# Engine queues of a seven-product FFN: written-out order from the seventh step on, data preparation over two steps, more squares on ScalarE

## The chip, the core and the metric

The program runs on one core of a Trainium2 chip. The metric is the device time of one execution in microseconds. Three runs of the kernel before gave 1070.18, 1069.46 and 1069.93 us, so the median is 1069.93 us.

## What is computed

From q, k, v of 6080 tokens by 256 channels an attention over channels is computed, and its output goes through two feed-forward blocks of width 2048. All inputs are float32.

```python
qn = q / (norm(q, axis=1) + 1e-06);  kn = k / (norm(k, axis=1) + 1e-06)
a = softmax(kn.T @ qn / tau)                 # 256 x 256
x = v @ a                                    # 6080 x 256
x = square(relu(x @ w_in)) @ w_out           # first block, 256 -> 2048 -> 256
h = x @ w_in2
return (h * clip(h + 3, 0, 6) / 6) @ w_out2  # second block
```

## The kernel before

**Head.** The scores of q and k are summed while their pieces arrive, then come norms, softmax and the transposed attention matrix (functions `score`, `scaled`, `transposed`, lines 558 to 677). The attention is not applied to the tokens: `attn_w` (line 475) multiplies it into the first block's input weights, so that the first block reads v itself.

**Steps.** The body is a list of 96 steps (`order`, line 911): two blocks (`ph`), six chunks of tokens (`c`), four units of 512 hidden channels (`u`) and two halves of a unit (`p`). In this document a step is named by its index i, from 0 to 95; "the seventh step" is i = 6, the first that works on unit 3 of chunk 0. A step (`step`, line 752) computes the hidden values of its half unit for one chunk as a 2 by 2 block product and, beside that, issues 24 matmuls that multiply the hidden values of the step before with the output weights (`out_mms`, line 696).

- Steps 0 to 5 (unit number under `PLAIN` = 3 in chunk 0) are plain: four blocks of two products each. A block's values go from PSUM (tile s) through relu into r (L802), are squared into h (by ScalarE, L804, or by VectorE, L806), and are split into a high and a low part g (ScalarE L108, VectorE L111).
- From step 6 on a step takes seven products, M1 to M7 in the code, of sums of weight blocks and sums of data blocks. Each product is three matmuls (L767: high by high, high by low, low by high). M1, M6, M7 and M4 add up in one PSUM bank x. After M1 its value is copied to m1 (trace: m), after M6 to u2 and after M7 to u3 (trace: u, twice in a step), all three by ScalarE (L108). So M6 can't start before copy m has read the bank, M7 not before the first copy u, and M4 not before the second.

```python
mul(x, M1, True); copy_act(m1, x)            # L867, L868
run(before); carry[0](); carry[1](); beside(0)
mul(pp, M2, True); add(h11, m1, pp); carry[2]()
mul(y, M5, True); pop(pops[0]); act(h11, "1"); beside(1)
mul(x, M6, False); copy_act(u2, x); hi11(); beside(2); lo11(); pop(pops[1]); beside(3)
mul(x, M7, False); copy_act(u3, x); add(h22, u3, y); act(h22, "2"); beside(4); pop(pops[2])
mul(x, M4, False); act_psum(h21, x); hi22(); beside(5); lo22(); pop(pops[3])
mul(y, M3, False); hi21(); beside(6); add(h12, u2, y); lo21(); pop(len(outs))
```

`carry` is what the step before left over: relu and square of its h12, and the split of it. `act(h, b)` (line 788) squares on ScalarE (relu L791, square L792) where the table `SQUARED_BY_ACT` names b for that step, and on VectorE otherwise (L794, one instruction).

**What sets the order.** Every engine runs its own queue in the order in which the instructions stand there. TensorE, SyncE and GpSimd have program order throughout. For ScalarE and VectorE a scheduler orders the queue up to step `MANUAL_FROM` - 1 (line 47, 8 before); from there on they too have program order (line 971), which is the order of the code above. `beside` (line 772) puts in work for later: `background` takes it from a list of tasks with due steps (weights that are converted, L138 and L139 on ScalarE, L126, L130, L142 and L134 on VectorE, then split into oh and ol; weight sums, tile wblk, with due steps `SUMS_DUE`), and `lane` holds the next chunk's data: eight slots b that are split in the same way, and four sums of blocks (tile blk) that VectorE makes (`FIRST` and `REST`, line 436; `add_lane`, line 444). `pops`, a table of four numbers, says how many of the 24 output matmuls go between the products; from `MANUAL_FROM` on it is `POPS_2`.

Of the kernel before, what the change touches and what calls it, by code (L numbers as in the profile page):

```python
# [43 lines left out]
LANE = (0, 1, 0, 1, 1, 1, 1)  # L44
DUE = (5, 4)
FINE = True
MANUAL_FROM = 8
LOAD_AHEAD = (2, 8, 8)
PLAIN = 3
PLAIN_POPS = (7, 6, 4, 7)  # L50
SUMS_DUE = (8, 10, 11)
HELD_BEHIND = {("t", 0, 0): 3, ("w", 0, 3): 3, ("s", 0): 5, ("s", 1): 5, ("s", 2): 5}
LANE_BEHIND = 5
SPLIT_FROM = 2
POPS = (3, 7, 5, 4)
POPS_2 = (3, 5, 6, 5)
AW_POPS = (1, 1, 1, 1)
FIRST_POPS = (6, 7, 4, 7)
SQUARED_BY_ACT = ("1", "012", "1", "012", "1", "1", "12", "12")


@with_exitstack
def tile_channel_attention_then_two_ffn(
# [21 lines left out]
    chunks, s = [], 0  # L85
# [117 lines left out]
    def run(fs):  # L203
        for f in fs:
            f()
# [53 lines left out]
    def front(n, k=0):  # L259

        for _ in range(n):
            t = tasks[k]
            t.steps.pop(0)()
            done[0] += 1
            if not t.steps:
                finished.add(tasks.pop(k).name)
                ensure_loads()
# [168 lines left out]
    FIRST, REST = (1, 2, 0, "sums", 5, 4), (3, 6)  # L436
# [7 lines left out]
    def add_lane(ph, c, slots, due):  # L444
        assert not lane
        b_ops.setdefault((ph, c), {})
        lane.extend(data_prep(data[ph, c], chunks[c][1], slots, new_slot(ph, c)))
        lane_due[0] = due
# [26 lines left out]
    def attn_w(u):  # L475

        if u == 1:

            ps = [psy.tile([P, 512], F32, tag=f"y0{dh}", name="aw") for dh in range(2)]
        else:  # L480
            ps = [bank([P, 512]) for _ in range(2)]

        def product(dh, eh):
            if u < SPLIT_FROM:
                return lambda: PE.matmul(ps[dh], e_sb[dh][:, eh], w1[u][:, eh], start=(eh == 0), stop=(eh == 1))

            def f():
                for k, (x, y) in enumerate(((0, 0), (0, 1), (1, 0))):
                    PE.matmul(ps[dh], e_parts[dh][x][:, eh], w1[u][y][:, eh], start=(eh, k) == (0, 0), stop=(eh, k) == (1, 2))
            return f  # L490

        r = blocks_tile("wblk" if u < 2 else "st")
        data["w", u] = r

        def take(dh):
            def f():
                ACT.activation(out=r[:, dh:4:2], in_=ps[dh].rearrange("p (g f) -> p g f", g=2),
                               func=AF.Copy, scale=rsum[:, dh:dh + 1])
            return f
        return [product(dh, eh) for dh in range(2) for eh in range(2)], [take(dh) for dh in range(2)]  # L500
# [16 lines left out]
    with tc.tile_pool(name="qk", bufs=4) as qkp, tc.tile_pool(name="at", bufs=1) as atp:  # L517
# [51 lines left out]
        for i, (wide, j, g) in enumerate(pieces):  # L569
            if i:  # L570
                load_piece(i + 3)
            t = loaded[i]
# [18 lines left out]
            for b in range(0, g - m, width):  # L591
                w = min(width, g - m - b)
# [56 lines left out]
        def transposed(dh):  # L649
            for eh in range(2):  # L650
                PE.transpose(t_ps[dh][:, eh], sc[dh][:, eh * P:(eh + 1) * P], ident)
            if dh == 0:
                copy_act(e_sb[dh], t_ps[dh])
            else:
                gate.append(DVE.tensor_scalar(out=e_sb[dh], in0=t_ps[dh], scalar1=1.0, scalar2=None, op0=ALU.mult).ins)
# [10 lines left out]
        front(1)  # L666
        scaled(1)
        row_sum(0)
        front(3)
        run(products[:2])  # L670
        transposed(1)
        ahead, take_next = attn_w(1)
        run(ahead[:1])
        parts[2]()
# [77 lines left out]
    def step(i, ph, c, u, p, before, outs, carry):  # L752
# [19 lines left out]
        def beside(at):  # L772
            parts = BESIDE if i < MANUAL_FROM else BESIDE_2
            k = -(-todo[0] * parts[at] // max(1, sum(parts[at:])))
# [103 lines left out]
        mul(y, M5, True)  # L878
        pops = AW_POPS if i == 0 else POPS if i < MANUAL_FROM else POPS_2
        pop(pops[0])  # L880
# [31 lines left out]
    LAST = 2 * NU - 1  # L912
# [21 lines left out]
    for i, (ph, c, u, p) in enumerate(order):  # L934
        at = i % (LAST + 1)
        nxt = (ph, c + 1) if c + 1 < NCHUNK else (1, 0) if ph == 0 else None
        if ph == 0 and c == 0:
            if i == 0:
                add_out_1(1, 3)
            elif p == 1 and u + 1 < NU and u:  # L940
                add_out_1(u + 1, i + 2)
        if i == 1:
            need(("half o", 0))
            last_lo[2] = last_lo[0].ins
            held.extend([("s", 0), ("w", 0, 1)])
        if (ph, c) == (0, 1) and at == 0:
            end = i
            for x, f in [(x, f) for x in range(NU) for f in (add_in_2, add_out_2)]:
                end += DUE[f is add_out_2]
                f(x, end)  # L950
        if nxt and at == (2 if i > LAST else 6):
            add_lane(*nxt, FIRST, i - at + LAST)
        if at == 0:
            assert not lane
        if ph == 0:
            need(("w", ph, u))
            if PLAIN <= u and c == 0:
                need(("t", 0, 0))
            if c == 1 and u < PLAIN:
                need(("s", u))  # L960
        outs = []
        if not prev:
            need(("w1", 1))
            take = take_next
            outs = [(f, None) for f in ahead[1:]]
        else:
            if prev[0][0] == 0 and prev[0][1] == 0:
                if i > 1:
                    need(("o", prev[0][2]))
            outs = out_mms(*prev[0], prev[1])  # L970
        if i == MANUAL_FROM:
            phase[0] = 2
            ctx.enter_context(tc.manual_schedule())

        if nxt and at == LAST:
            add_lane(*nxt, REST, i + 1)
        g, carry = step(i, ph, c, u, p, before, outs, carry)
        if i == 1:
            first_hi = last_lo[1]
        before = []  # L980
        if nxt and at == (0 if i > LAST else 5):
            if i <= LAST:
                need(("t", 0, 0))
            load_data(*nxt)
        if ph == 0 and c == 0 and p == 0 and u + 1 < NU:
            need(("w1", u + 1))
            if u:
                if u + 1 == SPLIT_FROM:
                    with tc.issue_after(first_hi), tc.issue_after(last_lo[2]):
                        split_e()  # L990
                products, before = attn_w(u + 1)
                run(products)
            else:
                before = take
            add_task(("w", 0, u + 1), lambda x=u + 1: in_1_steps(x), i + 2)
        if ph == 0 and c == 0 and u < PLAIN:
            if p == 0 and u == PLAIN - 1 < NU - 1:
                add_data("t", 0, 0, ("sums", 5, 4, 3, 6), i + 2)
            elif p == (u < NU - 1):
                add_weight_sums(u, SUMS_DUE[u])  # L1000
        if ph == 0 and c == NCHUNK - 1 and p:
            fetch_2("w", u)
        if prev and prev[0][0] == 0 and prev[0][1] == NCHUNK - 1 and prev[0][3]:
            fetch_2("o", prev[0][2])
        prev = ((ph, c, u, p), g)
# [38 lines left out]
```

## Time and profile before

| | |
|---|---|
| median of three runs | 1069.93 us |
| the profiled execution's own time | 1071.04 us |
| its span (first to last instruction) | 1069.3 us |
| TensorE busy with matmuls | 1061.4 us (99%) |
| VectorE busy | 898.6 us (84%) |
| ScalarE busy | 647.9 us (61%) |
| share of TensorE in the chain that ended last | 90% |
| granted TensorE clock, mean | 0.999 |

Busy time is the sum of the instructions of an engine. A matmul is shown as busy from its start to its modelled end, and the matmuls overlap, so a TensorE that is "99% busy" is read better by the starts of its matmuls: in steps without a wait they are 0.23 us apart. In the timeline PE is a matmul, PEld its weight load, ACT is ScalarE, DVE is VectorE; the first number is the start, the second the duration, in us.

### The profile page before, as it was taken

What the parts mean: (1) busy time and instruction counts of PE and PEld (TensorE: products, weight loads), DVE (VectorE), ACT (ScalarE), POOL (GpSimd) and SP (SyncE); (2) the same over time, 40 slices, a digit from 0 to 9 for tenths busy, and PEclk for the clock granted to TensorE, in tenths of its full rate; (3) what the DMA queues carried; (4) which work ended last, traced back from release to release, by engine and by line L of the source; (5) the groups of instructions that cost most, each with busy time, mean ns of one, the idle gap of its engine ahead of it and who ended that gap; (6) DMA issues with size and microseconds to landing.
All of it is one profiled execution on the core that took longest, in us unless ns stands there. A gap on an engine that the chain in (4) does not pass through costs nothing.

```text
span 1069.3 us, 12813 instructions
## 1 busy us (share of the span) xinstructions
PE 1061.4 (99%) x4602; PEld 865.2 (81%) x4602; DVE 898.6 (84%) x1523; ACT 647.9 (61%) x1125; POOL 9.4 (1%) x22
## 2 busy tenths in 40 slices
PE   9999999999999999999999999999999999999998
PEld 8778787888888888888888888888888888888886
DVE  6899988977887987887868988898898898898785
ACT  7698886666666666666565455455545555555443
POOL 0000000000000000000100000000000000000000
PEclk9999999999999999999999999999999999999999
DMA  9623130223132114115435002002002002001001
GB/s 359 245 80 118 59 117 21 89 81 96 60 108 79 49 60 142 35 60 197 148 130 184 1 0 78 1 1 78 1 1 78 1 1 64 15 0 39 1 1 39
DMA packets 33567, 78.03 MB, mean 73 GB/s; under 512 B 3296, under 2 KB 16864, under 8 KB 33504
## 3 DMA queue, kind: packets, MB, share of 16 engines
q1 hardware_dynamic: 27024, 57.49, 16.2%
q0 software_dynamic: 2304, 11.54, 3.2%
q10 hardware_dynamic: 4176, 8.19, 2.1%
q8 instruction: 36, 0.59, 0.2%
q14 instruction: 27, 0.22, 0.1%
HBM read 53.22 MB, written 23.99 MB: 72 GB/s over the span
## 4 chain that ended last, share of the span: by engine, by line
PE 90%; DVE 3%; ACT 3%; DMA 2%; issue 1%; ACTq 0%; SPq 0%; DVEq 0%
PE y L709 47%; PE s L767 41%; PE sc L559 2%; DMA q<-q_dram 1%; DMA w<-w_out_dram 1%; DVE g L111 0%; ACT g L108 0%; DVE h L806 0%; DVE ct L142 0%; DVE accq L114 0%; ACT cv L139 0%; ACT u L108 0%; ACT ct L138 0%; DVE cv L134 0%; DVE b L111 0%
## 5 line engine op out<-in xcount | busy, mean ns | idle before, releaser
L709 PE MATMUL y<-g,oh 128*128 128x506 f32 (+1 forms) x1536 | 508.8, 392 | 0.0
L767 PE MATMUL s<-b,wh 128*128 128x506 f32 (+1 forms) x1356 | 422.9, 393 | 1.1 <-ACT m L108 0.8
L111 DVE TENSOR_TENSOR g<-h,g 128x506 fp32r<-128x506 f32 (+1 forms) x384 | 262.0, 683 | 94.9 <-ACT g L108 85.3
L709 PEld LDWEIGHTS y<-g,oh 128*128 128x128 f32 x1536 | 289.4, 188 | 64.3 <-DVE g L111 0.4
L767 PEld LDWEIGHTS s<-b,wh 128*128 128x128 f32 x1356 | 254.6, 188 | 62.0 <-ACT u L108 2.2
L709 PE MATMUL y<-g,ol 128*128 128x506 f32 (+1 forms) x768 | 302.0, 393 | 0.0
L767 PE MATMUL s<-b,wl 128*128 128x506 f32 (+1 forms) x678 | 265.9, 392 | 0.1
L108 ACT ACTIVATE g<-h 128x506 fp32r<-128x506 f32 (+1 forms) x384 | 235.1, 622 | 30.0 <-DVE h L815 14.3
L108 ACT ACTIVATE u<-s 128x506 f32<-128x506 f32 (+1 forms) x180 | 107.0, 595 | 135.5 <-PE s L767 135.5
L709 PEld LDWEIGHTS y<-g,ol 128*128 128x128 f32 x768 | 144.6, 188 | 31.7
L767 PEld LDWEIGHTS s<-b,wl 128*128 128x128 f32 x678 | 127.9, 189 | 28.7 <-DVE wl L111 0.6
L114 DVE TENSOR_TENSOR h<-u,s 128x506 f32<-128x506 f32 (+1 forms) x180 | 122.1, 678 | 25.4 <-ACT u L108 22.4
L108 ACT ACTIVATE m<-s 128x506 f32<-128x506 f32 (+1 forms) x90 | 53.6, 595 | 111.5 <-PE s L767 110.5
L798 DVE SCALAR_TENSOR_TENSOR h<-r,h 128x506 f32<-128x506 f32 (+1 forms) x144 | 98.9, 687 | 4.9
L794 DVE SCALAR_TENSOR_TENSOR h<-h 128x506 f32<-128x506 f32 (+1 forms) x122 | 83.2, 682 | 1.4
L814 ACT ACTIVATE r<-s,three 128x506 f32<-128x506 f32 (+1 forms) x48 | 32.9, 686 | 60.2 <-PE s L767 59.8
L114 DVE TENSOR_TENSOR h<-m,s 128x506 f32<-128x506 f32 (+1 forms) x90 | 61.2, 680 | 8.6 <-PE s L767 2.9
L797 DVE TENSOR_SCALAR r<-h 128x506 f32<-128x506 f32 (+1 forms) x144 | 60.6, 421 | 1.7
L111 DVE TENSOR_TENSOR b<-blk,b 128x506 fp32r<-128x506 f32 (+1 forms) x85 | 57.7, 680 | 0.0
L108 ACT ACTIVATE b<-blk 128x506 fp32r<-128x506 f32 (+1 forms) x85 | 51.9, 616 | 0.0
L811 ACT ACTIVATE r<-s 128x506 f32<-128x506 f32 (+1 forms) x42 | 25.0, 595 | 38.7 <-PE s L767 36.4
L815 DVE SCALAR_TENSOR_TENSOR h<-r,s 128x506 f32<-128x506 f32 (+1 forms) x48 | 32.7, 681 | 10.4 <-ACT r L814 10.3
(96 smaller groups left out, 510.7 us busy)
## 6 DMA issues: line engine op xcount, KB each, us to landing
w<-w_in_dram SPq DMA_DIRECT2D x16, 512.0 KB, 5.6
w<-w_out_dram SPq DMA_DIRECT2D x16, 512.0 KB, 3.8
k<-k_dram SPq DMA_DIRECT2D x10, 512.0 KB, 7.0
blk<-vT_dram SPq DMA_DIRECT2D x8, 506.0 KB, 6.4
y<-y ACTq DMA_DIRECT2D x16, 253.0 KB, 2.7
blk<-y SPq DMA_DIRECT2D x8, 506.0 KB, 5.0
outT_dram<-y SPq DMA_DIRECT2D x15, 253.0 KB, 2.1
q<-q_dram SPq DMA_DIRECT2D x7, 512.0 KB, 7.7
```

Of the source, the lines that this page charges most:

```text
L108: return ACT.activation(out=out, in_=in_, func=AF.Copy)
L111: return DVE.tensor_tensor(out=out, in0=a, in1=b, op=ALU.subtract)
L114: DVE.tensor_tensor(out=out, in0=a, in1=b, op=ALU.add)
L559: return lambda: PE.matmul(s_ps[dh][:, :C], t["k"][:, b, dh * P:(dh + 1) * P], t["q"][:, b], start=first, stop=last)
L709: PE.matmul(y_ps[ph, c, b, e][:, :n], w[:, j, e * P:(e + 1) * P], x, start=start, stop=stop)
L767: PE.matmul(dst, w[:, a, rows], x, start=first and k == 0, stop=k == 2, skip_group_check=True)
L794: DVE.scalar_tensor_tensor(out=h, in0=h, scalar=0.0, in1=h, op0=ALU.max, op1=ALU.mult)
L797: DVE.tensor_scalar(out=r, in0=h, scalar1=3.0, scalar2=0.0, op0=ALU.add, op1=ALU.max)
L798: DVE.scalar_tensor_tensor(out=h, in0=r, scalar=6.0, in1=h, op0=ALU.min, op1=ALU.mult)
L811: ACT.activation(out=r, in_=x, func=AF.Relu)
L814: ACT.activation(out=r, in_=x, func=AF.Relu, bias=three)
L815: DVE.scalar_tensor_tensor(out=h, in0=r, scalar=6.0, in1=x, op0=ALU.min, op1=ALU.mult)
```

## The change

Four constants are changed, one function is called with other arguments, and one instruction of the head moves.

- `MANUAL_FROM` goes from 8 to 6: program order on ScalarE and VectorE, and `POPS_2`, hold from step 6.
- The first entry of `SUMS_DUE` goes from 8 to 5, and that task loses its mark in `HELD_BEHIND`: the weight sums of unit 0 come in steps 1 and 2.
- For chunk 1 all eight slots are put on the lane at step 6 and are due at step 8; before, six of the entries were due at the end of step 6 and the last two in step 7.
- `SQUARED_BY_ACT`: steps 4 and 5 square one more value on ScalarE, and so do steps 6 and 7 (h12, "0").
- In the head, two of three preparation instructions stand ahead of a pair of products and the transposes, and one behind.

```diff
-MANUAL_FROM = 8
+MANUAL_FROM = 6
...
-SUMS_DUE = (8, 10, 11)
-HELD_BEHIND = {("t", 0, 0): 3, ("w", 0, 3): 3, ("s", 0): 5, ("s", 1): 5, ("s", 2): 5}
+SUMS_DUE = (5, 10, 11)
+HELD_BEHIND = {("t", 0, 0): 3, ("w", 0, 3): 3, ("s", 1): 5, ("s", 2): 5}
...
-SQUARED_BY_ACT = ("1", "012", "1", "012", "1", "1", "12", "12")
+SQUARED_BY_ACT = ("1", "012", "1", "012", "12", "12", "012", "012")
...
         row_sum(0)
-        front(3)
+        front(2)
         run(products[:2])
         transposed(1)
+        front(1)
         ahead, take_next = attn_w(1)
...
         if nxt and at == (2 if i > LAST else 6):
-            add_lane(*nxt, FIRST, i - at + LAST)
+            add_lane(*nxt, FIRST if i > LAST else FIRST + REST, i - at + LAST + (i <= LAST))
...
-        if nxt and at == LAST:
+        if nxt and at == LAST < i:
             add_lane(*nxt, REST, i + 1)
```

In the changed file the lines from 672 on have numbers that are one higher, so L792 there is L791 here. Three places show how the queues move. Names keep their buffer numbers here, as several tiles would read alike without: m1, u2, u3, h11, h12 and h22 are the tiles of the code above, r the relu, s a PSUM bank, b a slot of the next chunk's data, blk the raw data, ct and cv steps of a weight's conversion, wblk weight sums.

ScalarE in step 6, before: from copy m to the second copy u.

```order
L108 ACTIVATE m1_1172<-s_1175 128x508
L108 ACTIVATE oh_1187<-cv_1227 128x512
L791 ACTIVATE r_1203<-h11_1168 128x508
L108 ACTIVATE u2_1173<-s_1175 128x508
L792 ACTIVATE h11_1168<-r_1203 128x508
L108 ACTIVATE b_1263<-blk_1165 128x508
L108 ACTIVATE g_1215<-h11_1168 128x508
L108 ACTIVATE u3_1174<-s_1175 128x508
```

The same stretch in the changed kernel, from the instruction behind copy m on.

```order
L803 ACTIVATE r_1190<-s_1132 128x508
L108 ACTIVATE g_1193<-h12_1056 128x508
L792 ACTIVATE r_1210<-h11_1178 128x508
L793 ACTIVATE h11_1178<-r_1210 128x508
L108 ACTIVATE b_1213<-blk_1173 128x508
L108 ACTIVATE u2_1183<-s_1185 128x508
L108 ACTIVATE g_1220<-h11_1178 128x508
L108 ACTIVATE oh_1222<-cv_1163 128x512
L138 ACTIVATE ct_1232<-w64_1171 128x512
L139 ACTIVATE cv_1233<-w64_1171 128x512
L108 ACTIVATE b_1238<-blk_1173 128x508
L108 ACTIVATE u3_1184<-s_1185 128x508
```

The relu of step 5's last value (r_1190) and its split now stand behind copy m; relu and square of h11 and a slot b stand between copy m and the first copy u, and five instructions between the two copies u, where two and three stood.

VectorE at the start of step 6, before: from the end of step 5's values to the sum h11 that reads copy m.

```order
L806 TENSOR_TENSOR h22_1050<-r_1109 128x508
L142 ISA ct_1226<-ct_1226,cv_1227 128x1024
L134 SCALAR_TENSOR_TENSOR cv_1227<-w64_1163,ct_1226 128x512
L111 TENSOR_TENSOR g_1112<-h22_1050,g_1112 128x508
L806 TENSOR_TENSOR h12_1048<-r_1180 128x508
L111 TENSOR_TENSOR b_1206<-blk_1165,b_1206 128x508
L111 TENSOR_TENSOR b_1209<-blk_1165,b_1209 128x508
L111 TENSOR_TENSOR g_1183<-h12_1048,g_1183 128x508
L114 TENSOR_TENSOR h11_1168<-m1_1172,s_1190 128x508
```

The same in the changed kernel.

```order
L111 TENSOR_TENSOR g_1120<-h22_1058,g_1120 128x508
L807 TENSOR_TENSOR h12_1056<-r_1190 128x508
L142 ISA ct_1162<-ct_1162,cv_1163 128x1024
L134 SCALAR_TENSOR_TENSOR cv_1163<-w64_1147,ct_1162 128x512
L114 TENSOR_TENSOR h11_1178<-m1_1182,s_1197 128x508
L111 TENSOR_TENSOR g_1193<-h12_1056,g_1193 128x508
```

Two slots b have left the stretch, and two conversion instructions (L142, L134) now stand between the square of step 5's last value and the sum h11.

VectorE from the second half of step 6 into step 7 in the changed kernel, up to the sum h11 of step 7.

```order
L111 TENSOR_TENSOR b_1251<-blk_1173,b_1251 128x508
L111 TENSOR_TENSOR blk_1173<-blk_1173 128x508 x2
L111 TENSOR_TENSOR g_1266<-h22_1181,g_1266 128x508
L111 TENSOR_TENSOR ol_1223<-cv_1233,oh_1222 128x512
L111 TENSOR_TENSOR blk_1173<-blk_1173 128x508
L114 TENSOR_TENSOR h12_1179<-u2_1183,s_1203 128x508
L111 TENSOR_TENSOR g_1280<-h21_1180,g_1280 128x508
L114 TENSOR_TENSOR wblk_456<-wblk_456 128x256
L114 TENSOR_TENSOR h11_1291<-m1_1295,s_1309 128x508
```

And before.

```order
L114 TENSOR_TENSOR wblk_428<-wblk_428 128x256
L111 TENSOR_TENSOR blk_1165<-blk_1165 128x508
L111 TENSOR_TENSOR wblk_428<-wblk_428 128x256 x2
L114 TENSOR_TENSOR h12_1169<-u2_1173,s_1196 128x508
L111 TENSOR_TENSOR g_1258<-h22_1171,g_1258 128x508
L111 TENSOR_TENSOR g_1274<-h21_1170,g_1274 128x508
L111 TENSOR_TENSOR b_1278<-blk_1165,b_1278 128x508
L794 SCALAR_TENSOR_TENSOR h12_1169<-h12_1169 128x508
L114 TENSOR_TENSOR h11_1288<-m1_1292,s_1305 128x508
```

The sum h12 of step 6 now stands behind the split of h22 and of an output weight (ol) and two more block sums, and its square has left VectorE.

## Rows read from the trace of the kernel before

**Rows 1.** The page's part 1: busy time of each engine.
```profile
PE 1061.4 (99%) x4602; PEld 865.2 (81%) x4602; DVE 898.6 (84%) x1523; ACT 647.9 (61%) x1125; POOL 9.4 (1%) x22
```

**Rows 2.** Windows cut at step starts: steps 1 to 5, then 6, 8, 9, 10, 11.
```profile
core 0: us, PE busy (x) PEld busy (x) DVE busy (x) ACT busy (x) POOL busy (x), PEclk, DMA share, GB/s
63.65:124.53 60.88, 60.88 (x265) 49.61 (x264) 57.07 (x104) 52.67 (x98) 0.00 (x0) 1.00 0.30 96
124.53:136.21 11.68, 10.87 (x47) 8.23 (x46) 11.61 (x21) 9.94 (x20) 0.00 (x0) 1.00 0.00 0
...
146.60:156.96 10.36, 10.36 (x47) 8.46 (x46) 8.10 (x15) 7.38 (x15) 0.00 (x0) 1.00 0.40 153
156.96:167.65 10.69, 10.63 (x47) 8.38 (x45) 8.78 (x17) 7.21 (x13) 0.00 (x0) 1.00 0.14 51
167.65:178.36 10.71, 10.61 (x46) 8.37 (x45) 8.80 (x16) 7.76 (x15) 0.00 (x0) 1.00 0.00 0
178.36:189.07 10.71, 10.62 (x47) 8.38 (x45) 9.79 (x18) 6.71 (x12) 0.00 (x0) 1.00 0.14 49
```

**Rows 3.** Waits of TensorE's weight loads: who for whom, total us, times, longest.
```profile
PEld s L767 <- ACT u L108: 2.2, 6, 0.5
PEld s L767 <- ACT m L108: 1.9, 3, 1.2
```

**Rows 4.** Timeline of ScalarE at the start of step 6.
```profile
125.52 1.65 ACT L108 ACTIVATE b<-blk 128x508 fp32r<-128x508 f32 x3
127.10 0.63 ACT L108 ACTIVATE g<-h 128x508 fp32r<-128x508 f32 x1
127.63 0.58 ACT L108 ACTIVATE m<-s 128x508 f32<-128x508 f32 x1
128.11 0.62 ACT L108 ACTIVATE oh<-cv 128x512 fp32r<-128x512 f32 x1
```

**Rows 5.** Timeline of TensorE: step 6's M6, the matmul that waited.
```profile
128.26 0.73 PE L767 MATMUL s<-b,wh 128*128 128x508 f32 x2 [0.81 <-ACT m L108]
```

**Rows 6.** Timeline of ScalarE in step 10.
```profile
172.82 0.66 ACT L138 ACTIVATE ct<-w 128x512 f32<-128x512 f32 x1
173.38 0.66 ACT L139 ACTIVATE cv<-w 128x512 int32<-128x512 uint32 x1
173.94 0.58 ACT L108 ACTIVATE u<-s 128x508 f32<-128x508 f32 x1
```

**Rows 7.** Timeline of TensorE in step 8: its start (M1), M7 and M4.
```profile
146.60 0.62 PE L767 MATMUL s<-b,wh 128*128 128x508 f32 x2
...
151.20 0.61 PE L767 MATMUL s<-b,wh 128*128 128x508 f32 x2
...
153.27 0.62 PE L767 MATMUL s<-b,wh 128*128 128x508 f32 x2
```

**Rows 8.** Timeline of ScalarE in step 8: copy m, then relu and square.
```profile
147.49 0.60 ACT L108 ACTIVATE m<-s 128x508 f32<-128x508 f32 x1 [0.27 <-PE s L767]
...
154.59 0.59 ACT L811 ACTIVATE r<-s 128x508 f32<-128x508 f32 x1 [0.41 <-ACT y L742]
155.21 0.63 ACT L812 ACTIVATE h<-r 128x508 f32<-128x508 f32 x1
```

**Rows 9.** Timeline of VectorE around the start of step 6.
```profile
123.80 0.68 DVE L806 TENSOR_TENSOR h<-r 128x508 f32<-128x508 f32 x1
124.40 0.68 DVE L142 CUSTOM_DVE_ANT_0 ct<-ct,cv 128x1024 uint16<-128x1024 uint16 x1
125.11 0.69 DVE L134 SCALAR_TENSOR_TENSOR cv<-w,ct 128x512 uint32<-128x512 uint32 x1
```

**Rows 10.** Timeline of TensorE in the head: the products behind the transposes.
```profile
53.24 1.98 PE L485 MATMUL s<-w,e 128*128 128x512 f32 x4 [0.30 <-DVE e L655]
```

**Rows 11.** Windows at the program's end, after the last matmul.
```profile
1064.70:1067.10 2.40, 0.00 (x0) 0.00 (x0) 0.42 (x1) 0.38 (x1) 0.00 (x0) 1.00 0.63 216
1067.20:1069.20 2.00, 0.00 (x0) 0.00 (x0) 0.00 (x0) 0.00 (x0) 0.00 (x0) 0.50 0.00 0
```

## The prediction

> **What bounds the kernel now.** I read the page's busy times first: TensorE is busy for 1061.4 of 1069.3 us [rows 1]. All that the other engines do can only cost time where a matmul waits for it, so the next views are the windows cut at the steps and the waits of the weight loads. Of the body's 96 steps only a few hold a wait. Steps 1 to 5 are full: 60.88 us long, 60.88 busy [rows 2]. A full step of seven products takes 10.36 us, as step 8 does; step 6 takes 11.68 and steps 9, 10 and 11 take 10.69, 10.71 and 10.71 [rows 2], which is 1.32 + 0.33 + 0.35 + 0.35 = 2.35 us too much. The waits behind this are weight loads that wait for ScalarE's copies m and u [rows 3]. Two places show the kind. In step 6 three slots b (1.65 us) and a split g stand ahead of copy m, which starts at 127.63 [rows 4]; M6 starts at 128.26, after an idle TensorE [rows 5]. In step 10 two conversion instructions stand ahead of the second copy u [rows 6]. So the bound is TensorE, and what counts elsewhere is only how far ScalarE's copies are from the bank they read. Against full steps there is not more than these 2.35 us to win.
>
> **The clock that I sum against.** In an undisturbed step TensorE starts M1 at 0, M7 at +4.60 (151.20 - 146.60) and M4 at +6.67 [rows 7], and copy m starts at +0.89 [rows 7, 8]. From M7 to M4 there are 2.07 us. ScalarE's instructions of this size, back to back, start about 0.48 us apart after a copy or relu from PSUM (127.63 to 128.11), 0.53 after a split [rows 4], 0.56 after a conversion [rows 6]; one that needs the result of the one just before starts 0.62 later (154.59 to 155.21) [rows 8]. VectorE's start 0.60 apart, 0.71 where the one before is needed, and last 0.68 [rows 9]. A copy that ended at 128.21 let a matmul start at 128.26, and that restart cost another 0.1, as the pair took 0.73 in place of 0.62 [rows 4, 5, 7].
>
> **Step 6 as now ordered.** The chain goes by the order of the queues shown above. Copy m +0.89; the relu of step 5's last value behind it +1.37, until +1.95; VectorE squares it +1.99, then the two conversions +2.59 and +3.30, and only then the sum h11, +3.91 to +4.59. ScalarE's relu of h11 starts +4.63, the square +5.26, the slot b +5.78, and the first copy u +6.3 to +6.9. M7 is due at +4.60 and starts at +6.94: 2.34 late, with the restart 2.45. Then g, oh, ct, cv and b stand between the two copies (0.5 each, 0.56 for the conversions), so that the second starts at +9.47 and M4 at +10.1; M4 was due 2.07 + 0.1 after M7, at +9.1. That is 1.0 late, 1.1 with the restart. Step 6: **+3.55 us** against a full step.
>
> **Step 7.** It starts 13.92 after step 6. Counted from step 6's start, the sum h22 comes at +10.2 on VectorE; behind it two conversions, a slot b (which waits for its high part until +12.7), two sums blk, the split of h22, an output weight, another sum blk: the sum h12 runs from +16.3 to +17.0. Relu and square of h12 are ScalarE's now: +17.0 and +17.7, its split +18.3; relu and square of h11 +18.8 and +19.45, a slot b +20.0, copy u +20.5 to +21.1. M7 was due at 13.92 + 4.60 = +18.5 and starts at +21.1: 2.6 late, with the restart **+2.7 us**. The second copy u then has only g and b in front and is in time.
>
> **Step 8** has squares on VectorE again, but begins with relu and square of step 7's h12 on ScalarE behind a VectorE that is some 2 us late; by the same count its first copy u ends 0.6 after M7 is due: **+0.7 us**. In step 9 I find copy m done just as M6 is due: 0, at most 0.2.
>
> **What is taken away.** The wait of step 6 is no more (no slot b is ahead of copy m). In steps 9, 10 and 11 the instructions that stood ahead of the late copies have moved (a split wh, conversions); with the same spacing the copies have 0.3 us or more in hand. **-2.35 us.**
>
> **What costs nothing.** The weight sums of unit 0 (four small sums, two splits on each engine, under 3 us of VectorE) come in steps 1 and 2, and two squares of steps 4 and 5 go to ScalarE: both lie where TensorE is never late [rows 2], and a value has most of a plain step (11 us) before its matmuls; if that cover were gone, the wait would be what is left of those 3 us. The head: TensorE idles 0.30 us for VectorE's copy of the attention matrix [rows 10], which is now one instruction earlier; step 0 then still waits for ScalarE's splits of the first weights, so 0, with -0.3 as the other end. On SyncE one weight load moves ahead of chunk 2's data; nothing needs either before step 10. GpSimd's queue is the same, and so is TensorE's but for where the 24 matmuls of steps 6 and 7 stand.
>
> **Sum.** 3.55 + 2.7 + 0.7 - 2.35 = +4.6 us. The profiled execution took 1071.04 us (span 1069.3), 1.1 over the median of 1069.93. So the changed kernel should take 1071.04 + 4.6 = 1075.6 in such an execution, and 1069.93 + 4.6 = **1074.5 us** in the median. The lower end of the mechanism takes VectorE as never behind: step 6 then keeps its 3.5, step 7 only ScalarE's own chain (copy m, relu, square, split, relu, square, b, copy u: ends at +5.4, so 0.85 late, 0.95 with the restart), step 8 none: 3.55 + 0.95 - 2.35 = +2.15, 1072.1. The upper end gives steps 8 and 9 another 1 us each: 1076.5.
>
> **A page that speaks against the change.** In this trace the granted clock of TensorE is 1.00 (2.4 GHz) through all waits of the body, of which the longest is the 0.81 us of [rows 5]; after the last matmul it is 1.00 for some 2.4 us and then 0.50, which is 1.2 GHz [rows 11]. The waits that I forecast, 2.3 and 2.6 us, are longer than any in the body before, and about as long as that last spell. The Trainium skill, page "TensorE: Matmul & The Clock Gate", section "HAM oscillation — how this bites in real kernels", says that idle gaps between bursts of matmuls make the clock fall, so that the next burst starts slow. The end of the trace agrees that the clock falls behind the work; no row shows it within the body. The sum by rows is 1074.5; with that rule it would be the third rival's.
>
> **Rivals.**
> 1. *The queues flow and the waits vanish: faster.* VectorE is busy 11.61 of 11.68 us in step 6 [rows 2] and loses work in steps 4 to 7; fewer slots stand ahead of copy m. If the copies come in time, 2.35 us go: 1067.6. It decides at one point: ScalarE must reach the first copy u by +4.0, so the sum h11 must be done by about +1.7. Against it stands the order itself: h11 is behind a relu that is behind copy m, and behind two conversions. Chance 0.06.
> 2. *Only step 6 pays.* VectorE catches up in step 6's long wait; step 7 pays 0.9 us or less, step 8 nothing, and 9 to 11 are clean: +1.2 to +2.1, 1071.1 to 1072.0. For it: both engines idle before step 6. Against it: three sums blk and two conversions are in front of h12 in that very step. Chance 0.13.
> 3. *The clock falls in step 6 or 7.* Matmuls at half the pace for the rest of such a step: behind M4 of step 6 there are 3.7 us of work, which would take 3.7 more, less what the slower pace gives step 7's late copies (up to 2.7): +1 to +3.7 on top, 1075.5 to 1078.2. Chance 0.07.
>
> **How the numbers follow.** The forecast, 1072.1 to 1076.8, has 0.74. It and rival 3 are slower by more than 0.2%, which is 2.1 us and about what a measurement of this kernel can tell from no change: 0.81. Rival 2 is the same: 0.13. Rival 1 is faster: 0.06. The range from 1071.0 to 1077.2 takes in the forecast, half of rival 2 and most of rival 3, and leaves out rival 1.
>
> **What would show it.** In the changed profile step 6 should be some 13.9 us long and step 7 some 13.1, with weight loads that wait for copy u by 2.3 and 2.6 us and one by 1.0; steps 9 to 11 should take 10.4 each; VectorE should be idle for about 3 us ahead of the square of step 5's last value. I am wrong if steps 6 and 7 stay under 11 us, if the wait falls on a copy m, or if the clock column shows less than 1.00 there.

## The result, and the profile after

The changed kernel takes 1077.14 us (median of six executions, 1076.72 to 1077.82), the kernel before 1069.93 (1069.46 to 1070.18): ratio 1.0069, interval 1.0056 to 1.0082. It is slower, as forecast, but by 7.2 us where 4.6 were forecast. The forecast was 1074.5; the median lies at the very edge of the range (1071.0 to 1077.2), and the ratio on the median of before gives 1077.3, just outside it.

The profiled execution took 1077.80 us (span 1076.0), which is 6.76 more than the one before. Page, part 1, which answers to [rows 1]: busy times are nearly the same, so TensorE does no more work, it waits.

```profile
PE 1062.0 (99%) x4602; PEld 866.0 (80%) x4602; DVE 896.2 (83%) x1519; ACT 652.4 (61%) x1131; POOL 9.3 (1%) x22
```

Windows of the changed kernel cut at its steps, to be read against [rows 2] (the columns are those): steps 1 to 5 together, then 6 to 12 one by one.

```profile
63.55:124.44 60.89, 60.89 (x265) 49.62 (x264) 55.77 (x103) 53.69 (x99) 0.00 (x0) 1.00 0.30 96
124.44:138.37 13.93, 10.93 (x46) 8.31 (x45) 9.20 (x16) 9.70 (x18) 0.00 (x0) 1.00 0.13 38
138.37:153.61 15.24, 12.21 (x47) 9.52 (x46) 11.70 (x21) 12.47 (x23) 0.00 (x0) 0.89 0.00 1
153.61:163.96 10.35, 10.35 (x46) 8.45 (x45) 7.57 (x14) 8.21 (x15) 0.00 (x0) 1.00 0.59 201
163.96:174.32 10.36, 10.36 (x46) 8.38 (x45) 8.82 (x16) 7.32 (x14) 0.00 (x0) 1.00 0.14 53
174.32:184.68 10.36, 10.36 (x47) 8.45 (x46) 8.84 (x16) 7.34 (x13) 0.00 (x0) 1.00 0.00 0
184.68:195.03 10.35, 10.35 (x46) 8.45 (x45) 9.25 (x16) 6.17 (x12) 0.00 (x0) 1.00 0.20 60
195.03:206.17 11.14, 10.63 (x46) 8.38 (x45) 10.48 (x20) 7.22 (x15) 0.00 (x0) 1.00 0.24 87
```

Against the kernel before: head -0.10, step 6 +2.25, step 7 +4.85 (before 10.39, from 136.21 to 146.60 [rows 2]), steps 9 to 11 together -1.04, step 12 +0.79 (before 10.35; its start and end there are 189.07 and 199.42). That is +6.7, the whole difference of the spans. The head's share means little: in the eleven profiles of kernels with the new head, step 1 starts anywhere from 63.01 to 63.95 us. In step 7 the granted clock, the third figure from the right, is 0.89.

Timeline of TensorE: M7 and M4 of step 6, then step 7 from M7 on, then M3 of step 12.

```profile
131.41 0.72 PE L768 MATMUL s<-b,wh 128*128 128x508 f32 x2 [2.18 <-ACT u L108]
134.57 0.72 PE L768 MATMUL s<-b,wh 128*128 128x508 f32 x2 [0.81 <-ACT u L108]
146.17 0.73 PE L768 MATMUL s<-b,wh 128*128 128x508 f32 x2 [3.03 <-ACT u L108]
...
147.45 0.62 PE L710 MATMUL y<-g,ol 128*128 128x508 f32 x1
147.87 1.05 PE L710 MATMUL y<-g,oh 128*128 128x508 f32 x2
...
204.22 0.72 PE L768 MATMUL s<-b,wh 128*128 128x508 f32 x2 [0.51 <-DVE h L114]
```

All waits of steps 6 and 7 are for a copy u. Behind 147.45 a matmul takes 0.42 us in place of 0.23. Two windows of step 7, the wait for M7 and the slow spell behind it:

```profile
142.75:147.35 4.60, 1.57 (x7) 1.00 (x6) 3.05 (x7) 4.52 (x9) 0.00 (x0) 1.00 0.00 0
147.45:150.75 3.30, 3.30 (x9) 2.64 (x8) 2.37 (x6) 2.12 (x5) 0.00 (x0) 0.50 0.00 0
```

The wait itself passes at a clock of 1.00; the fall to 0.50 (1.2 GHz) comes 1.3 us after M7 has started. Eight matmuls at 0.42 in place of 0.23 are 1.5 us, and step 7 is longer by 3.2 (M7 late) + 0.1 (restart) + 1.5.

### The profile page after: what moved, and what is told of

The parts are those of the page before. It is cut to its first block, busy times and chain, and to the rows that moved or that the text cites. A ratio compares the mean times of both kernels' runs of the same rounds, so it can differ in the third digit from the quotient of the medians.

```text
span 1076.0 us, 12814 instructions
## 1 busy us (share of the span) xinstructions
PE 1062.0 (99%) x4602; PEld 866.0 (80%) x4602; DVE 896.2 (83%) x1519; ACT 652.4 (61%) x1131; POOL 9.3 (1%) x22
## 4 chain that ended last, share of the span: by engine, by line
PE 93%; DVE 3%; ACT 2%; DMA 1%; issue 1%; ACTq 0%; SPq 0%; DVEq 0%
PE y L710 48%; PE s L768 42%; PE sc L559 2%; DMA q<-q_dram 1%; PE s L489 1%; DVE h L114 0%; DVE g L111 0%; DVE accq L114 0%; ACT h L793 0%; DVE blk L111 0%; ACT r L792 0%; ACT g L108 0%; ACT sq L588 0%; ACT b L108 0%; DVE ct L142 0%
## 5 line engine op out<-in xcount | busy, mean ns | idle before, releaser
L816 DVE SCALAR_TENSOR_TENSOR h<-r,s 128x506 f32<-128x506 f32 (+1 forms) x48 | 32.6, 680 | 10.3 <-ACT r L815 10.2
```

The source lines that it names most:

```text
L816: DVE.scalar_tensor_tensor(out=h, in0=r, scalar=6.0, in1=x, op0=ALU.min, op1=ALU.mult)
```

## The experiments

Each was timed beside the kernel before on the same chip, whose median was 1070.0 to 1070.2 us there. Steps are named as before.

### What the slow clock costs: matmuls in the gap

```diff
+        if i == 7:
+            for _ in range(8):
+                PE.matmul(pp, wh[:, 0, :P], b_slots[1][:, 0, :n], ...)
         mul(x, M7, False)
```

> The changed kernel with eight extra matmuls on TensorE ahead of M7 of step 7, whose sums nobody reads; nothing else is touched. Theory: the slow clock behind M7 of step 7 comes from TensorE's 3.2 us of idleness and is a cost of its own, beside the wait. The eight matmuls (8 x 0.23 = 1.8 us) lie inside that idle time, so M7 starts when it did (7.8 us after the start of step 7), the granted clock stays 1.00 there, step 7 falls from 15.24 to about 13.7 us, and step 8, which had caught up while the clock was low, gets 0 to 0.8 us of wait: 0.8 to 1.6 us less than the changed kernel's 1077.1, so 1075.5 to 1076.3. Rival 1: the clock falls all the same, because of both waits together or by something else: no change, 1077.1 within 0.4. Rival 2: the extra matmuls delay M7 itself: more, up to 1078.9.

Measured: 1077.51 us (ratio 1.007, 1.0055 to 1.0085). Windows of steps 6 to 9:

```profile
123.94:137.86 13.92, 10.93 (x46) 8.30 (x45) 9.19 (x16) 9.69 (x18) 0.00 (x0) 1.00 0.12 38
137.86:151.56 13.70, 12.74 (x54) 9.80 (x53) 10.56 (x19) 11.08 (x21) 0.00 (x0) 1.00 0.01 1
151.56:162.72 11.16, 10.64 (x47) 8.38 (x46) 8.54 (x15) 9.46 (x18) 0.00 (x0) 1.00 0.55 186
162.72:173.20 10.48, 10.48 (x47) 8.39 (x46) 8.95 (x16) 7.43 (x14) 0.00 (x0) 1.00 0.14 52
```

The profile does what the theory says: M7 starts 7.82 us into step 7 (7.80 without the extra matmuls), the clock stays 1.00, step 7 takes 13.70. But step 8 now pays 0.80 and step 9 0.12: the slow spell had given the copies time to catch up. The spell is 1.54 us in its step and 0.6 net. The median does not show even that, but it mixes two kinds of execution: 1076.95 and 1077.09 us at a mean clock of 1.000 and 0.999 (the second is the profiled one), 1077.93 and 1078.05 at 0.998 and 0.997, so the extra matmuls did not hold the clock up every time. Nor is a lower clock a longer time in the changed kernel itself: two executions with a mean clock of 0.996 took 1076.97 and 1077.07 us, the four with 0.998 took 1076.72 to 1077.82. With no slow spell the kernel still takes 1077.0, so the clock is not what makes it slower; the late copies are. Step 8's 0.80 answers to the +0.7 of the prediction.

### Two conversions from ahead of the sum h11

```diff
-            parts = BESIDE if i < MANUAL_FROM else BESIDE_2
+            parts = BESIDE if i < MANUAL_FROM else BESIDE_2 if i != 6 else (0, 1, 2, 3, 2, 2, 2)
```

> The changed kernel with the two conversion instructions of VectorE moved from ahead of the sum h11 of step 6 to behind it. Theory: they are 1.3 us of the 2.34 us by which M7 of step 6 is late, so that wait falls to about 1.0 to 1.3 us, step 6 from 13.93 to 12.6 us; the sum h22 comes that much earlier, and step 7's wait stays as long as it was or gets shorter. Total 1.3 to 2.9 us less (the larger figure if the clock then stays 1.00 in step 7), 1074.2 to 1075.8. Rival: VectorE has no slack from there to the sum h12, so what step 6 gains is lost again as a longer wait in step 7: 1077.1 within 0.5.

Measured: 1076.46 us (ratio 1.006, 1.0045 to 1.0075). Step 6 takes 12.60 us, 1.33 less, just the two instructions; step 7 takes 15.26, as long as in the changed kernel, with the same slow spell. By the steps 1.3 us are gained, by the medians 0.7, which is less than the theory's range and a little more than the rival's. The steps decide against the rival (nothing is paid back in step 7), and the larger gain of the theory did not come. VectorE's two instructions ahead of h11 are on the path of step 6 at full length.

### All squares of steps 6 and 7 on VectorE

```diff
-SQUARED_BY_ACT = ("1", "012", "1", "012", "12", "12", "012", "012")
+SQUARED_BY_ACT = ("1", "012", "1", "012", "12", "12")
```

> The changed kernel with the squares of steps 6 and 7 on VectorE again, one instruction each, in place of relu and square on ScalarE; the order stays written out. Theory: relu and square of h11 stand in ScalarE's queue ahead of the first copy u (1.15 us in step 6), and in step 7 those of step 6's h12 as well (two instructions each, about 1.2 us). M7 of step 6 comes about 1.1 us earlier less the 0.7 of VectorE's own square if the split needs it first; step 7's M7 1.5 to 2.4 us earlier, so that its wait falls to about 1 us and the clock stays 1.00. Together with the 1.5 us of the slow clock that is 3 to 5 us less than 1077.1: 1072 to 1074. Rival: VectorE, not ScalarE, sets both waits, and with more squares it is later still: 1077 or more.

This takes more from ScalarE than the change gave it: in the kernel before, these steps already squared h11 and h22 on ScalarE ("12"), and the change added h12 ("0"). Here all three go to VectorE.

Measured: 1073.93 us (ratio 1.0037, 1.0024 to 1.005), in the range expected, but by another way in step 6. ScalarE there, both copies u and what stands between:

```profile
127.84 0.58 ACT L108 ACTIVATE u<-s 128x508 f32<-128x508 f32 x1
129.91 0.63 ACT L108 ACTIVATE g<-h 128x508 fp32r<-128x508 f32 x1 [1.49 <-DVE h L795]
130.44 0.61 ACT L108 ACTIVATE oh<-cv 128x512 fp32r<-128x512 f32 x1
130.96 0.65 ACT L138 ACTIVATE ct<-w 128x512 f32<-128x512 f32 x1
131.51 0.66 ACT L139 ACTIVATE cv<-w 128x512 int32<-128x512 uint32 x1
132.08 0.61 ACT L108 ACTIVATE b<-blk 128x508 fp32r<-128x508 f32 x1
132.59 0.57 ACT L108 ACTIVATE u<-s 128x508 f32<-128x508 f32 x1
```

The first copy u is in time and M7 too. But the split g waits for VectorE's square, and everything behind it waits as well: M4 starts 2.46 us late, the clock falls behind it, and step 6 takes 14.49 us. The gain is all in step 7, 10.99 us in place of 15.24, as forecast: relu and square of h12 and of h11 no longer stand ahead of its first copy u. How much of it belongs to h12, the one square that the change moved in each of these steps, this run does not tell.

### The order alone undone

```diff
-MANUAL_FROM = 6
+MANUAL_FROM = 8
```

> The changed kernel with only the order undone: the scheduler orders steps 6 and 7 as before, program order from step 8; the other three edits stay. Theory: the order is what costs in steps 6 and 7 (2.25 and 4.84 us longer than before), since the scheduler puts the first copy u ahead of the square of h11. Then steps 6 and 7 together take 22 to 23 us in place of 29.2, the waits of steps 9 to 11 stay gone, step 12's 0.8 us stays: 1077.1 - 6 to 7 = 1070 to 1071. Rival 1: the squares that moved to ScalarE and the spread data cost in any order: 1073 or more. Rival 2: with the fixed order gone the scheduler uses the lighter VectorE and step 6's old wait goes too: under 1069.4.

Measured: 1069.91 us (ratio 0.9997, 0.9987 to 1.0007). Steps 6, 7 and 12:

```profile
124.34:135.10 10.76, 10.66 (x46) 8.38 (x45) 10.76 (x20) 8.62 (x17) 0.00 (x0) 1.00 0.00 0
135.10:145.66 10.56, 10.56 (x46) 8.38 (x45) 6.68 (x12) 9.58 (x19) 0.00 (x0) 1.00 0.24 67
...
187.10:198.23 11.13, 10.62 (x46) 8.38 (x45) 10.47 (x20) 7.22 (x15) 0.00 (x0) 1.00 0.24 87
```

The theory holds: one constant is worth 7.2 us. ScalarE's queue in step 6 shows why: the first copy u stands between relu and square of h11, and four instructions, that square among them, are between the copies.

```profile
127.81 0.63 ACT L792 ACTIVATE r<-h 128x508 f32<-128x508 f32 x1 [1.21 <-DVE h L114]
128.34 0.58 ACT L108 ACTIVATE u<-s 128x508 f32<-128x508 f32 x1
128.82 0.62 ACT L793 ACTIVATE h<-r 128x508 f32<-128x508 f32 x1
...
130.89 0.58 ACT L108 ACTIVATE u<-s 128x508 f32<-128x508 f32 x1
```

The constant switches three things in steps 6 and 7: who orders the queues, `POPS` to `POPS_2`, and `BESIDE` to `BESIDE_2`, the table that spreads the background work over a step. No run separates them. `POPS_2` puts M7 two output matmuls earlier, which at 0.23 us each is 0.46 of the 2.37 us by which M7 of step 6 is late; the run with the copies first, below, keeps `POPS_2` and has no wait in step 6. Program order with the old tables was not run.

### The order alone, on the kernel before

```diff
-MANUAL_FROM = 8
+MANUAL_FROM = 6
```

> The kernel before with MANUAL_FROM 6 in place of 8 and nothing else. Theory: the written-out order is what costs, and without the lighter lane it costs a little more than in the changed kernel. One more slot b stands ahead of the first copy u of step 6: M7 about 2.85 us late, M4 1.0 us, step 6 some 14.4 us. In step 7 the squares of h12 are VectorE's and four sums of blocks stand ahead of h12 and h11, so that the first copy u ends near +22.9 us from the start of step 6 where M7 is due at +19.0: 3.9 us late, step 7 some 14.4 us (more by up to 1.6 if the clock falls). The small waits of steps 9 to 11 stay (10.7 us each), step 12 stays clean. Against the kernel before: +2.75 in step 6, +4.0 in step 7, 0 to 0.8 in step 8: 1076 to 1079, middle 1077. Rival: the order is harmless as long as no squares move and the data are not spread: under 1073.

Measured: 1080.22 us (ratio 1.0091, 1.0076 to 1.0106), above the range expected. Step 6 takes 15.11 us, 0.7 over the working, which is the clock (mean 0.89; it falls 1.0 us after M7 has started). Step 7 takes 17.10, in which M7 starts 8.95 us after the step's start (4.35 late) and the clock is 0.80. M7 and M4 of step 6 came as worked out within 0.1 us, M7 of step 7 0.45 us later than that; the clock came on top in both steps. So the changed kernel's other edits give back some 3 us of what its order costs.

### The spread of the second chunk's data undone

```diff
-            add_lane(*nxt, FIRST if i > LAST else FIRST + REST, i - at + LAST + (i <= LAST))
+            add_lane(*nxt, FIRST, i - at + LAST)
...
-        if nxt and at == LAST < i:
+        if nxt and at == LAST:
```

> The changed kernel with only the spread of the second chunk's data undone: six of the entries are due at the end of step 6 again, the last two in step 7. Theory: under the written-out order every slot b that is issued ahead of a copy u, and every sum blk ahead of the sum h12, is paid at its full length. One slot more ahead of the first copy u of step 6: 13.93 + 0.5 = 14.4 us. Four VectorE instructions more ahead of h12 and h11: step 7's M7 2.4 us later, 15.24 + 2.4 = 17.6 us. Together +2.9: 1080 within 0.8. So the spread is worth some 3 us in the changed kernel, and squares and sums little. Rival: VectorE has slack there, and the spread is worth nothing: 1077.1 to 1077.7.

Measured: 1079.41 us (ratio 1.0089, 1.0075 to 1.0102). Step 6 takes 14.46 us and step 7 17.92, where 14.4 and 17.6 were worked out. (The lane holds seven slots b and the four block sums, not eight slots.) Step 6 is as the theory has it, one more slot. For step 7 the agreement is luck: its M7 is 4.66 us late, 1.46 more than in the changed kernel and not 2.4 more, and the slow spell behind it lasts about twice as long, which adds some 1.2. The sum h12 does come 2.0 us later (+18.84 from the start of step 6, against +16.86), but 0.5 of that is already in step 6. Under the written-out order the spread is worth 2.3 us by the medians. The run above has the order without the spread, the squares, the early sums and the new head; it takes 0.8 us more than this one, which is what the last three are worth together here.

### Written-out order with the copies first

```diff
-        act(h11, "1"); beside(1); mul(x, M6, False); copy_act(u2, x); hi11(); beside(2); lo11(); pop(pops[1]); beside(3)
-        mul(x, M7, False); copy_act(u3, x); add(h22, u3, y); act(h22, "2")
+        mul(x, M6, False); copy_act(u2, x); act(h11, "1"); pop(pops[1])
+        mul(x, M7, False); copy_act(u3, x); add(h22, u3, y); act(h22, "2"); hi11(); beside(1); beside(2); lo11(); beside(3)
```

(for steps 6 and 7 alone)

> The changed kernel, still in written-out order from step 6, but in steps 6 and 7 relu and square of h11 are issued behind the first copy u, and the split of h11 and what stands beside it (three groups of conversions and slots b) behind the second copy u and h22. Theory: it is only the place of these instructions in ScalarE's queue ahead of the two copies u that made M7 and M4 late, not their amount. So M7 and M4 of step 6 come in time (copy u at +3.8 us, the second by +6.4), step 6 takes 10.4 to 10.8 us, the clock stays 1.00; VectorE then reaches the sum h12 some 3 us earlier, and step 7 is at most 0.5 us late: 10.4 to 11.0. Step 12's 0.8 us stays. Together 1069.5 to 1071. Rival: the work itself is too much for VectorE in steps 6 and 7 (spread data, conversions), so that the wait reappears for h12 or h11 in step 7 or 8: 1073 or more.

Measured: 1077.99 us (ratio 1.0069, 1.0052 to 1.0085). Windows of steps 6 and 7:

```profile
124.84:135.23 10.39, 10.39 (x47) 8.46 (x46) 4.73 (x8) 7.24 (x13) 0.00 (x0) 1.00 0.17 50
135.23:154.28 19.05, 13.78 (x46) 10.19 (x45) 15.36 (x28) 14.53 (x28) 0.00 (x0) 0.82 0.00 1
```

For step 6 the theory is shown: with the copies first it is a full step without a wait. For the total the rival holds: VectorE does only 4.73 us of work in step 6 and 15.36 in step 7. What was moved back now stands ahead of M4's relu, of copy m and of h12, and step 7 takes 19.05. Placing the copies is half of the task; the work that is moved must fit behind them.

### Where step 12's wait comes from, and a kernel that beats both

With the scheduler's order in steps 6 and 7, the weight sums were put back (SUMS_DUE 8 and the mark in HELD_BEHIND).

> The changed kernel with the scheduler's order for steps 6 and 7 (as in the run that undid the order alone) and with the weight sums of unit 0 put back to step 8 and behind their mark. Theory: moving these sums early is what cleared steps 9 to 11 and, by bringing the whole list of background tasks forward, what put a weight split ahead of a relu in step 11 and so made step 12 wait 0.8 us. So steps 9, 10 and 11 take 10.7 us each again and step 12 10.35: 1.05 - 0.78 = +0.3 us, 1070.2 within 0.4; step 6 may get up to 1.0 us of its old wait back, then 1071.2. Rival: the spread of the second chunk's data or the squares cleared steps 9 to 11 and cause step 12's wait: steps 9 to 11 stay at 10.36, step 12 at 11.13, 1069.9.

Measured: 1070.95 us (ratio 1.0008, 0.9998 to 1.0017). Steps 9 to 11 take 10.90, 10.74 and 10.71 again, step 12 10.35, step 6 11.46. So the early sums cleared steps 9 to 11 and made step 12's wait. ScalarE in step 11 of the changed kernel, at the place where in the kernel before the relu followed copy u:

```profile
190.41 0.57 ACT L108 ACTIVATE u<-s 128x508 f32<-128x508 f32 x1
193.27 0.63 ACT L108 ACTIVATE st<-wblk 128x512 fp32r<-128x512 f32 x1 [2.29 <-DVE wblk L134]
193.81 0.58 ACT L812 ACTIVATE r<-s 128x508 f32<-128x508 f32 x1
```

The list of background work has moved up, and the split st waits 2.29 us for a conversion on VectorE with the relu behind it. VectorE in turn waits for the split that follows:

```profile
195.59 0.69 DVE L111 TENSOR_TENSOR g<-h,g 128x508 fp32r<-128x508 f32 x1 [0.96 <-ACT g L108]
...
203.49 0.67 DVE L114 TENSOR_TENSOR h<-u,s 128x508 f32<-128x508 f32 x1
```

From there to 203.49 VectorE has no gap, so M3 waits for that sum. The test moves st behind the relu:

```diff
-            parts = BESIDE if i < MANUAL_FROM else BESIDE_2
+            parts = BESIDE if i < MANUAL_FROM else BESIDE_2 if i != 11 else (1, 0, 2, 2, 1, 2, 4)
```

> The run that undid the order alone (the changed kernel, scheduler's order in steps 6 and 7), and in step 11 one background instruction is issued later: ScalarE's split st of a weight sum stands behind the relu of M4's bank and the split of h22 in place of ahead of them, and VectorE's split g ahead of its split st. Theory: in step 11 that st waits for a VectorE conversion and holds the relu behind it for 1.2 us; VectorE's g, st and the sum h12 follow 0.6 us later, and since VectorE has no gap from there to step 12's sum h22, M3 of step 12 waits 0.8 us. So step 12 falls from 11.13 to 10.5 us, and the time from 1069.9 to 1069.3, 0.7 below the kernel before. Rival: step 12's wait comes from the weight sums that lie in step 12 itself: it stays 11.13 and the time 1069.9.

Measured: 1068.86 us (eleven executions; ratio 0.9988, 0.998 to 0.9997), faster than both kernels, though by little: 1.3 us below the kernel before, and the interval ends just short of 1. Steps 6, 11 and 12:

```profile
123.91:134.52 10.61, 10.61 (x47) 8.38 (x46) 10.61 (x20) 8.46 (x17) 0.00 (x0) 1.00 0.00 0
...
176.14:186.49 10.35, 10.35 (x47) 8.45 (x45) 9.55 (x17) 7.23 (x14) 0.00 (x0) 1.00 0.15 51
186.49:196.84 10.35, 10.35 (x46) 8.46 (x45) 10.25 (x20) 6.52 (x13) 0.00 (x0) 1.00 0.29 104
```

Step 12's wait is gone altogether, not only 0.6 of it.

### The clock once more

To the run with the squares on VectorE the same eight matmuls were added, ahead of M4 of step 6.

> The run with the squares of steps 6 and 7 on VectorE, with eight extra matmuls on TensorE ahead of M4 of step 6, whose sums nobody reads. There TensorE waits 2.5 us for the second copy u and its clock falls to one half right behind. Theory: with the gap partly filled the granted clock stays 1.00 and step 6 falls from 14.49 to 12.9 us; but the slow spell had also given ScalarE and VectorE time, so that step 7 (10.99) takes 0.8 to 1.5 us more: 0.1 to 0.8 us less than that run's 1073.9, so 1073.1 to 1073.8. Rival 1: the slow spell is a cost of its own in full: 1072.3. Rival 2: it falls all the same, or the extra matmuls delay M4: 1073.9 or more.

Measured: 1074.69 us (ratio 1.0039, 1.0024 to 1.0055): no gain, 0.8 more than without them. In the profile, which is the slowest of its four executions, step 6 takes 12.95 us at a clock of 1.00, but step 7 14.03: its M7 then waits 1.83 us and the clock falls there. The slow spell was moved, not removed. The four executions show what a spell is worth here: mean clock 1.000 and 0.999 at 1074.09 and 1073.70 us, 0.998 at 1075.80 and 1075.29, so some 1.6 us. That price does not carry over: without the extra matmuls one execution with a mean clock of 0.999 took 1074.06 us, and those with 0.997 took 1073.91 to 1074.08.

### The head alone, and the old head

The head's edit alone on the kernel before:

> The kernel before with only the head's edit: two of three preparation instructions ahead of the products and the transposes, one behind. Theory: it moves at most an idle time of 0.3 us; step 1 starts within 0.3 us of the 63.65 us of the kernel before, and the time is the same as before within 0.3 us, 1070.0. Rival: it costs some 0.4 us, which would be why the changed kernel's median rose by 7.2 us where its steps account for 6.8: 1070.4.

Measured: 1071.92 us (ratio 1.0014, 1.0005 to 1.0023), more than either case. The head is not where it is lost: step 1 starts at 63.53. Step 6 takes 12.51 us in place of 11.68, and there ScalarE has a slot b and the square of h11 ahead of copy u:

```profile
129.18 0.63 ACT L792 ACTIVATE r<-h 128x508 f32<-128x508 f32 x1 [0.70 <-DVE h L114]
129.78 0.63 ACT L108 ACTIVATE b<-blk 128x508 fp32r<-128x508 f32 x1
130.31 0.61 ACT L793 ACTIVATE h<-r 128x508 f32<-128x508 f32 x1
130.83 0.57 ACT L108 ACTIVATE u<-s 128x508 f32<-128x508 f32 x1
```

One instruction in the head makes the scheduler order the queues anew up to step 7. That is 0.8 of 1.8 us. The two profiled executions (1072.15 and 1071.04 us) differ by only 1.1: the profile before lies 0.9 above the median of 1070.11 beside this run, this one 0.2 above its own, which is the other 0.7. Whether the head itself takes anything was tried with the old head in the fastest kernel:

> The run with step 11's split moved, with the head of the kernel before (all three preparation instructions ahead of the products and the transposes). The median less the profile's time from the start of step 1 to that of step 13 is what head and tail take: 1070.0 - 135.8 = 934.2 us for the kernel before and 1080.2 - 145.9 = 934.3 for it with the order alone changed, but 934.9 to 935.3 for five kernels with the new head (without the squares, with the scheduler's order, with sums put back, head alone, step 11 moved). Theory: the new head costs 0.6 to 0.9 us. Then steps 1 to 12 take 133.9 us as in that run, and the time is 1068.0 to 1068.3, 0.16 to 0.2% under the kernel before. Rival 1: head and tail differ by chance: 1068.9 again. Rival 2: the scheduler, which orders steps 0 to 7 anew when the head changes, gives back a wait in step 6 or 7: steps 1 to 12 above 134.5 us, 1069 or more.

Measured: 1068.89 us (ratio 0.9989, 0.998 to 0.9998), with steps 1 to 12 at 134.0 us: rival 1, the head's edit costs nothing here. What the expectation was built on stays open: median less steps 1 to 12 is 934.2 us for the kernel before and 934.9 here too, with the same head. The one profile of before is 1.1 us above its median. Up to 0.6 of that can be its head, as step 1 starts at 63.65 us there and at 63.08 here; the rest would lie in its steps, and no second profile of it shows that.

## Why the prediction was right and wrong

The direction and the mechanism were right: late copies u, in steps 6 and 7. Three terms failed: the start of the sum h12 in step 7, worked out 0.56 us too early; the clock, held at 1.00 in the sum, which fell in step 7; and the weight sums, put at nothing, which cost 0.79 us in step 12.

**Step 6, +3.55: right to 0.02.** From the step's start the copies u begin at +6.34 and +9.48 (forecast +6.3 and +9.47), M7 at +6.97 (+6.94) and M4 at +10.13 (+10.1). VectorE was idle 3.09 us ahead of the square of step 5's last value, as said. Walking the queues in their order with start-to-start spacings from [rows 4], [rows 6], [rows 8] and [rows 9] was enough.

**Step 7, +2.7: right in mechanism, too small in size.** Two terms failed. The first is the sum h12, forecast at +16.3. VectorE up to it:

```profile
135.02 0.68 DVE L114 TENSOR_TENSOR h<-u,s 128x508 f32<-128x508 f32 x1
...
137.57 0.69 DVE L111 TENSOR_TENSOR b<-blk,b 128x508 fp32r<-128x508 f32 x1 [0.54 <-ACT b L108]
...
141.30 0.67 DVE L114 TENSOR_TENSOR h<-u,s 128x508 f32<-128x508 f32 x1
```

h22 came at +10.58 (forecast +10.2), since VectorE had two conversions and a slot's low part ahead of it. Relu and square of h22 and the next slot's high part on ScalarE came as much later, so VectorE took up that slot at +13.13 in place of +12.7; the two block sums behind it took 0.1 more than counted, and h12 came at +16.86. M7 was 3.2 us late in place of 2.6. The second is the clock: **the prediction held the forecast and rival 3 apart, with 0.74 and 0.07, though the forecast's own waits were what would bring the clock down.** It fell, for eight matmuls, 1.5 us in step 7, 0.6 net. The prediction had named a clock under 1.00 in these steps as a sign of being wrong, and step 7 shows 0.89. Rival 3 had the price from the work left behind M4 of step 6 (1 to 3.7 us); it came in step 7 and ended of itself sooner. That the measured time lies in that rival's range (1075.5 to 1078.2) is in part luck, as step 12 brought more than the clock did net.

**Step 8, +0.7: came to nothing**, and the run with matmuls in the gap shows why: with the clock at 1.00 it is 0.80. The slow spell had replaced it. **Step 9**: 0, and 0.12 in that run; forecast 0 to 0.2.

**What is taken away, -2.35: right.** Steps 9 to 11 take 10.36, 10.36 and 10.35; copy m no longer holds M6 of step 6. What cleared steps 9 to 11 was the early weight sums, not the order: with the order alone they take 10.7 each.

**What costs nothing: wrong for the weight sums.** The prediction looked at steps 1 and 2, where they were put, and at their cover there. It did not ask what moves up in the list that they left: step 12 paid 0.79. The squares of steps 4 and 5 cost nothing (steps 1 to 5 take 60.89 us, 60.88 before), and in the fastest kernel the head makes no difference (1068.86 and 1068.89 us). On the kernel before, the head's edit alone costs 1.8 us, 0.8 of it because the scheduler then orders step 6 otherwise, which the prediction did not consider.

The sum: +4.6 forecast; +0.6 (h12), +1.5 (clock), -0.7 (step 8), +0.8 (step 12), -0.1 (head) make +6.7. The medians differ by 7.2, as the profile before stands 1.1 over its median and that after 0.7. One bound was not carried over: the upper end is worked out as 1076.5, and the chance of 0.74 is given for a forecast up to 1076.8.

**The page that spoke against the change.** The Trainium skill, page "TensorE: Matmul & The Clock Gate", section "HAM oscillation — how this bites in real kernels", has gaps between bursts make the clock fall, so that the next burst starts slow. The trace agrees in part: in step 7 the clock falls behind the wait (0.50 from 147.45 on), but the burst starts at full pace and slows 1.3 us later, and behind the waits of step 6 it does not fall. By that rule alone the spell would be a full cost; the filled gap shows 0.6 of 1.5 net.

## What to carry to other kernels

An engine with an in-order queue is late by what stands ahead of the one instruction that others wait for: count the instructions between the bank's last matmul and the copy that frees it, at their start-to-start spacing, and put nothing there that itself waits for a third engine. When work is moved out of a list, look at the steps from which the rest of the list then moves up, not only at where it went. Where a forecast itself contains waits longer than any in the trace, the clock's reaction belongs into the sum, not into a rival, and so does what the engines behind catch up in a slow spell.

## What was not expected of the hardware

The length of a wait does not tell whether the clock falls. In step 6 of the changed kernel TensorE idled 2.18 and then 0.81 us, and the clock stayed 1.00; with the squares on VectorE one wait of 2.28 us, and in the run with extra matmuls there one of 1.83 us, brought it to 0.50. Nor does it tell when: after 3.03 us the changed kernel's M7 of step 7 still starts at full pace (its pair takes 0.73 us), while after 3.01 us in the run with the copies first M7's pair takes 1.22 us, as the clock has already fallen. The lines show M4 of step 6 with the squares on VectorE, M7 of step 7 with the extra matmuls ahead of M4, and M7 of step 7 with the copies first:

```profile
133.21 0.73 PE L768 MATMUL s<-b,wh 128*128 128x508 f32 x2 [2.28 <-ACT u L108]
...
144.07 0.75 PE L768 MATMUL s<-b,wh 128*128 128x508 f32 x2 [1.83 <-ACT u L108]
...
145.79 1.22 PE L768 MATMUL s<-b,wh 128*128 128x508 f32 x2 [3.01 <-ACT u L108]
```

And executions of one program differ in it: of the four with the extra matmuls ahead of M4, two show a mean clock of 0.999 or more and two 0.998.
